# A spectral mixer with an MLP: stages one and two issued from lists of single steps, and the scale's sums in one bank

## The chip, the cores and the metric

The kernel runs on one core of a Trainium2 chip. The metric is device time in microseconds, from one execution of the whole program. The times of several runs are given by their median; the profile is of one execution, whose own time stands beside its span.

## The reference

The input x has 2048 rows of 512. Six vectors (sa, ca, ga, sb, cb, gb) of 512 come from silu(c) @ w_mod, c being one vector of 512. Two residual blocks follow, cut here to what matters:

```python
h = layernorm(x) * (1 + ca) + sa
X = rfft2(h) * (w_r + 1j * w_i)            # over the 2048 rows and the 512 columns
x = x + ga * irfft2(X)
h = layernorm(x) * (1 + cb) + sb
a = mish(h @ w1 + b1)                      # 512 to 1376
x = x + gb * (a @ w2)                      # 1376 to 512
```

All inputs and outputs are float32.

## The kernel before, in words

The row index is 16p + n for the 128 partitions p and 16 tiles n, so that one tile n holds 128 rows. The two-dimensional transform is made of small matmuls in three stages, and the MLP belongs to the third.

**Stage one** (lines 357 to 439) goes over the 16 tiles. For tile n it takes the row transform of x by four products with kr (`p1_row`, the products on L269), subtracts the mean (`p1_mean`, L284, VectorE), scales by the inverse deviation and splits the result into a high and a low part (`p1_cast`, L291 to L300 on ScalarE; the low part on GpSimd, L298, for odd n up to 13, else on VectorE in `p1_low`, L307). Then `p1_col` does the first part of the column transform in three parts of three matmuls (L314 to L316), the third of which needs the low part, and `p1_save` (L320) puts it into `a_sb`. The column matrices come as float32 and are split by `p1_split` (L261 on ScalarE, L262 and L263 on GpSimd). The statistics are `norm_sums` (L183, L184), `first_guess` (L188, L189) and `first_scale` (L196). Two buffers in PSUM of each of four tags (A, B, C, D) go round: the row products use A and B, the column products C.

Before the first tile, the factor 1 + ca is worked into kr: `gate` makes silu(c) (L377 to L380), `scale_sums` (L322 to L326) multiplies the columns of w_mod (`wmc`) with it, in four banks of 128 equal columns, and `scale_rows` (L328 to L331) makes four slices `krs` = kr * sum + kr on VectorE, each from its own bank. The shift sa is summed at the end of stage one (`shift_sum`, L176) and goes through the row transform in `shift_rows` (L336 to L350).

**Stage two** (lines 643 to 697) goes over 17 groups of up to four of the 64 frequency columns; group 0 is a special one (`z_...`). A group is transposed on TensorE (`p2_in`, L539), copied to SBUF (L542), shifted (L550, GpSimd), multiplied by the constant kf (`p2_mul`, L559), multiplied pointwise with the filter (`p2_prod`: two lane copies on ScalarE L590 and L591, GpSimd L592, VectorE L593), added (`p2_add`, L599), multiplied by kv (`p2_out`, L608) and stored (`store_d`, L450 to L458) by three engines. The last group's product is on VectorE alone (L583 to L586). Between the groups VectorE makes column sums of w_mod (`mod_late`, L176), and the gate ga goes through memory (`flat`, `spread`, L99 and L103) into kiv (`mod_gate`, L635, GpSimd).

**Stage three** (from line 1163) has the last two transforms (`p3_col`, L859 and L860; `p3_row`, L869) and the MLP, with its weights and activations as high and low parts and a seven-product scheme for two-by-two blocks (`up`, L974 and L991; `down`, L1091).

**What sets the order.** The kernel schedules by hand: every engine does its instructions in the order in which the program issues them, and DMAs go into the queue of the engine that issues them (mostly SyncE, SP). In stages one and two this order is written as loops with fixed leads. In stage three each step is put into a `Plan` with a key, the steps are sorted by key, and the list `ORDER` says in which order the sorted steps are issued (L1165 to L1176).

Of the kernel before, what the change touches and what calls it, by code (L numbers as in the profile page):

```python
# [12 lines left out]
P = 128  # L13
S, D, F = 2048, 512, 1376
L = D // 2 + 1
N2 = 16
# [17 lines left out]
ORDER = (  # L34
# [49 lines left out]
def tile_spectral_block(ctx: ExitStack, tc: tile.TileContext, x_d, w1_d, b1_d, w2_d,  # L84
# [157 lines left out]
    def load_all(n):  # L242
        load_xt(n)
        load_x(n)
        load_m(n)

    def load_rest():
        nc.sync.dma_start(kf, kf_d)
        nc.sync.dma_start(wz, wz_d)
        for i in range(4):  # L250
            nc.sync.dma_start(wqa[:, i], wq_d[i])
            if i == 1:
                nc.sync.dma_start(kv, kv_d)
                nc.sync.dma_start(kw, kw_d)
                nc.sync.dma_start(kiv, ki_d)
                nc.sync.dma_start(b1n[:, 0:NF - 1], b1_d[0:(NF - 1) * P].rearrange("(f p) -> p f", p=P))
                nc.sync.dma_start(b1n[0:F - (NF - 1) * P, NF - 1:NF], b1_d[(NF - 1) * P:F].unsqueeze(1))

    def p1_split(n):
        m = mt(n)  # L260
        nc.scalar.copy(m[:, 0, 0:256], mraw[:, n, :])  # L261
        nc.gpsimd.tensor_tensor(m[:, 1, 0:256], mraw[:, n, :], plain(m[:, 0, 0:256]), op=ALU.subtract)  # L262
        nc.gpsimd.tensor_scalar(m[:, :, 256:384], plain(m[:, :, 128:256]), -1.0, 0.0,  # L263
                                op0=ALU.mult, op1=ALU.add)
# [12 lines left out]
    def row_sums():  # L277
        ps = bank("D")
        row_products(ps, lambda j: ones)
        nc.scalar.copy(kb, ps)  # L280
# [6 lines left out]
    def p1_cast(n):  # L287
        c = st["c", n]
        one = rstd[:, n:n + 1]
        gh, gl = buf("g1", F32R), buf("g2", F32R)  # L290
        if n in POOL_LOW:  # L291
            g = buf("t")
            if n == 1:
                nc.scalar.activation(gh, c, AF.Copy, scale=one)
            nc.scalar.activation(g, c, AF.Copy, scale=one)
            if n > 1:
                nc.scalar.copy(gh, g)
            nc.gpsimd.tensor_tensor(gl, g, plain(gh), op=ALU.subtract)  # L298
        else:
            nc.scalar.activation(gh, c, AF.Copy, scale=one)  # L300
        st["g", n] = gh, gl

    def p1_low(n):
        c = st.pop(("c", n))
        if n not in POOL_LOW:
            gh, gl = st["g", n]
            nc.vector.scalar_tensor_tensor(gl, c, rstd[:, n:n + 1], plain(gh), op0=ALU.mult, op1=ALU.subtract)  # L307
# [1211 lines left out]
```

## Time and profile before

| | us |
|---|---|
| median of 3 runs (368.21 to 368.68) | 368.21 |
| the profiled execution's own time | 368.36 |
| its span | 366.6 |
| TensorE busy (PE) | 358.6 |
| VectorE (DVE) | 302.5 |
| ScalarE (ACT) | 266.9 |
| GpSimd (POOL) | 78.3 |

The span runs from the first to the last instruction; the time around it is outside of what the profile shows. TensorE's busy time is made of modelled ends of pipelined matmuls; PEld is its loading of weights, which goes on beside it. In the rows below, L followed by a number is a line of the kernel above, and the arrow in brackets names what ended a wait.

### The profile page before, as it was taken

The page shows a single profiled execution, that of the slowest core. Times are in us where ns is not written, and L with a number is a line of the kernel's source. Part 1 is how long each engine was busy: PE and PEld are TensorE (multiplying, and loading weights), DVE is VectorE, ACT ScalarE, POOL GpSimd, SP SyncE. Part 2 cuts the span into 40 slices and gives each one's busy share as a digit, 9 for nine tenths or more (in the row PEclk, how much of TensorE's full clock was granted, in tenths as well). Part 3 has the DMA queues.
Part 4 walks back from the last instruction along what each step waited for, and adds up shares of the span by engine and source line. Part 5 has one row for each costly group of instructions (what it writes and reads, how often), then busy time and mean ns, then how long its engine had stood idle before and what let it go on. Part 6 is the DMA issues. An engine that isn't in the chain of part 4 may idle for free.

```text
span 366.6 us, 7820 instructions
## 1 busy us (share of the span) xinstructions
PE 358.6 (98%) x2666; PEld 333.9 (91%) x2666; DVE 302.5 (83%) x752; ACT 266.9 (73%) x601; POOL 78.3 (21%) x126
## 2 busy tenths in 40 slices
PE   8999999998999999999999999999999999999994
PEld 8999977777999998798999999999999999999994
DVE  1898968888889799998994777998759977887995
ACT  1798879996799999998773878766577753555650
POOL 0588738786011001100002101004100000000000
PEclk9999999999999999999999999999999999999998
DMA  7999997678498776899888877786989678863133
GB/s 254 383 349 377 331 373 250 219 185 305 142 327 254 236 256 230 278 306 322 248 225 292 276 236 200 207 276 206 281 301 243 215 229 266 227 219 62 59 57 115
DMA packets 54343, 89.96 MB, mean 245 GB/s; under 512 B 7552, under 2 KB 20960, under 8 KB 54048
## 3 DMA queue, kind: packets, MB, share of 16 engines
q1 hardware_dynamic: 49728, 74.65, 62.0%
q0 software_dynamic: 2416, 7.87, 9.0%
q10 hardware_dynamic: 2160, 6.95, 6.0%
q8 instruction: 21, 0.34, 0.4%
q14 instruction: 18, 0.15, 0.1%
HBM read 68.21 MB, written 17.57 MB: 234 GB/s over the span
## 4 chain that ended last, share of the span: by engine, by line
PE 84%; ACT 5%; DVE 4%; DMA 2%; POOL 1%; issue 1%; ACTq 1%; SPq 0%; DVEq 0%; POOLq 0%
PE bank L1091 25%; PE bank L991 22%; PE bank L974 6%; PE bank L269 4%; PE bank L869 4%; PE bank L859 3%; PE bank L860 3%; PE bank L1037 3%; PE bank L314 3%; PE bank L1087 3%; DMA hT<-in_B_w_dram 2%; PE bank L1103 2%; PE bank L316 1%; PE bank L315 1%; PE bank L325 1%
## 5 line engine op out<-in xcount | busy, mean ns | idle before, releaser
L991 PE MATMUL bank<-hT,wr 128*128 128x256 f32 x360 | 51.6, 283 | 0.0
L991 PEld LDWEIGHTS bank<-hT,wr 128*128 128x128 f32 x360 | 47.3, 191 | 0.6
L991 PE MATMUL bank<-hB,wr 128*128 128x256 f32 x318 | 46.6, 285 | 0.0
L991 PEld LDWEIGHTS bank<-hB,wr 128*128 128x128 f32 x318 | 41.9, 191 | 0.9
L1143 POOL DMA_DIRECT2D x<-modr x7 | 6.3, 898 | 140.5 <-DVE modr L1142 84.7
L1091 PE MATMUL bank<-w2a,ah 128*128 128x256 f32 x161 | 35.1, 283 | 0.0
L917 DVE TENSOR_TENSOR al<-buf,ah 128x512 fp32r<-128x512 f32 (+1 forms) x45 | 30.1, 668 | 5.7 <-ACT ah L916 4.7
L1091 PE MATMUL bank<-w2b,ah 128*128 128x256 f32 x147 | 32.2, 283 | 0.0
L916 ACT CAST ah<-buf 128x512 fp32r<-128x512 f32 (+1 forms) x45 | 27.0, 602 | 4.5 <-DVE buf L1061 2.6
L1091 PEld LDWEIGHTS bank<-w2a,ah 128*128 128x128 f32 x161 | 27.0, 191 | 0.4
L859 PE MATMUL bank<-kc,d 128*128 128x128 f32 x128 | 24.9, 276 | 0.5 <-ACT d L452 0.5
L1091 PEld LDWEIGHTS bank<-w2b,ah 128*128 128x128 f32 x147 | 24.9, 191 | 0.3
L860 PE MATMUL bank<-kc,d 128*128 128x128 f32 x128 | 24.8, 275 | 0.0
L974 PE MATMUL bank<-hB,wr 128*128 128x512 f32 x96 | 24.4, 393 | 0.0
L1091 PE MATMUL bank<-w,ah 128*128 128x256 f32 x112 | 21.5, 284 | 0.0
L314 PE MATMUL bank<-buf,mring 128*128 128x512 f32 x48 | 20.6, 430 | 0.2 <-DVE buf L307 0.2
L974 PEld LDWEIGHTS bank<-hB,wr 128*128 128x128 f32 x96 | 17.3, 189 | 3.1
L859 PEld LDWEIGHTS bank<-kc,d 128*128 128x128 f32 x128 | 19.4, 192 | 0.7 <-ACT d L452 0.7
L860 PEld LDWEIGHTS bank<-kc,d 128*128 128x128 f32 x128 | 19.5, 192 | 0.0
L1091 PEld LDWEIGHTS bank<-w,ah 128*128 128x128 f32 x112 | 17.7, 191 | 0.6
L608 PEld LDWEIGHTS bank<-kv,a_sb 128*128 128x128 f32 x126 | 15.5, 192 | 2.8 <-issue 2.2
L788 POOL DMA_DIRECT2D turned<-x x16 | 8.9, 568 | 42.1 <-DVE x L782 42.1
(310 smaller groups left out, 1098.2 us busy)
## 6 DMA issues: line engine op xcount, KB each, us to landing
wr<-w_S SPq DMA_DIRECT2D x60, 256.0 KB, 4.0
wr<-w_A SPq DMA_DIRECT2D x45, 256.0 KB, 3.8
w_S<-hT SPq DMA_DIRECT2D x20, 256.0 KB, 2.9
x<-in_A_x_dram SPq DMA_DIRECT2D x16, 256.0 KB, 4.7
xring<-in_x_t_dram SPq DMA_DIRECT2D x16, 256.0 KB, 4.6
w_A<-wr SPq DMA_DIRECT2D x15, 256.0 KB, 3.1
x<-modr POOLq DMA_DIRECT2D x7, 512.0 KB, 5.5
out_dram<-x SPq DMA_DIRECT2D x7, 512.0 KB, 3.8
```

The lines of the kernel that those rows point to most:

```text
L269: nc.tensor.matmul(pgv[:, j], data(j), krs[:, j, :].rearrange("p (c q) -> p c q", c=2), start=True, stop=True)
L314: nc.tensor.matmul(pa, m[:, a, 0:128], g, start=(i == 0), stop=False)
L608: nc.tensor.matmul(pd[:, i * P:(i + 1) * P], y[:, i * P:(i + 1) * P], kv[:, 0:128], start=True, stop=True)
L859: nc.tensor.matmul(o, dj[:, 0:128], kc[0][:, n, :], start=True, stop=False)
L860: nc.tensor.matmul(o, dj[:, 64:192], kc[1][:, n, :], start=False, stop=True)
L869: nc.tensor.matmul(px[:, j * P:(j + 1) * P], e[:, j * P:(j + 1) * P], kiv[:, j, :], start=True, stop=True)
L916: nc.scalar.copy(h, r)
L917: nc.vector.tensor_tensor(l, r, plain(h), op=ALU.subtract)
L974: nc.tensor.matmul(ups[i, t, f], ring[t, a][:, p, b, :], sides[int(a[2]) - 1][:, :, q, b, :], start=(a[2] == "1" and b == 0 and n == 0), s ...
L991: nc.tensor.matmul(o, w[:, p, k, :], h[:, q, k, :], start=(first and n == 0), stop=(last and n == 5), skip_group_check=True)
L1037: nc.tensor.matmul(ups[i, 0][:FL], w1s[:, p, u, :], sides[u // 2][:, :, q, u % 2, :], start=(u == 0 and p + q == 0), stop=(u == 3 and p == ...
L1091: nc.tensor.matmul(out_ps[b][n][:, 256 * half:256 * half + 256], a[p][:, e], w2[t][q][:, r], start=(t == 1 and half == 0 and i == 0), stop ...
```

## The change

Four things are done.

1. Stages one and two become plans like stage three. The loops are cut into single steps (a load, a split's three parts, one part of a column product, one lane copy, one half of a store), which are put into `opening` and `middle` in the old order, roughly, and issued in the order of two new lists of 302 and 268 steps. The work of each engine stays on it, except for item 3.
2. Stage three gets a new list as well, for the same 1187 steps. Of these, half move by six places or fewer.
3. The scale's sums: one bank and 64 equal columns for each of the four slices in place of four banks of 128. The 1 is added once, to the four sums together (`scale_ones`), and the four slices are plain products with it, two on VectorE and two on ScalarE.
4. `shift_pick`, a reduction of the identity, is a step of its own.

The core of the diff, without the lists and without steps that are only cut out of their functions:

```diff
-    def scale_sums(ks, ps):
-        for k in ks:
-            for j in range(4):
-                nc.tensor.matmul(ps[j][:, 0:P], wmc[:, k, j * P:(j + 1) * P], sc[:, k:k + 1].to_broadcast([P, P]),
-                                 start=(k == 0), stop=(k == 3))
-    def scale_rows(ps):
+    def scale_sums(k):
+        if k == 0:
+            st["one"] = bank("C")
+        ps = st["one"]
         for j in range(4):
-            nc.vector.scalar_tensor_tensor(krs[:, j, :], kr[:, j, :], ps[j][:, 0:1], kr[:, j, :],
-                                           op0=ALU.mult, op1=ALU.add)
+            nc.tensor.matmul(ps[:, 64 * j:64 * j + 64], wmc[:, k, j * P:(j + 1) * P], sc[:, k:k + 1].to_broadcast([P, 64]),
+                             start=(k == 0 and j == 0), stop=(k == 3), skip_group_check=True)
+
+    def scale_ones():
+        ps = st.pop("one")
+        st["one"] = one = small.tile([P, 4], F32, name="one")
+        nc.vector.tensor_scalar(one, ps[:, 0:256:64], 1.0, None, op0=ALU.add)
+
+    def scale_row(j):
+        one = st["one"][:, j:j + 1]
+        if j % 2:
+            nc.scalar.activation(krs[:, j, :], kr[:, j, :], AF.Copy, scale=one)
+        else:
+            nc.vector.tensor_scalar(krs[:, j, :], kr[:, j, :], one, None, op0=ALU.mult)
...
+        def run(self, which):
+            steps = [e[2:] for e in sorted(self, key=lambda e: e[:2])]
+            places = [[int(n) for n in run.split("-")] for run in ORDERS[which].split()]
...
+    with tc.manual_schedule():
+        opening.run(0)
...
+        middle.run(1)
...
-    plan.run()
+    plan.run(2)
```

The places in the new lists that the prediction speaks of, by engine (`a > b` means that a is issued before b):

- SP: wmc's first quarter > sc > the other quarters > kr > x 0 > xt 0 > xt 1. At the end of stage one: three of wqa's four loads > kiv > kf > wz.
- VectorE, stage one: `scale_ones` > `scale_row` 0 and 2 > `norm_sums` 0 > ... > `norm_sums` 3 > `shift_pick` > `p1_mean` 2.
- TensorE, stage one: `p1_col` 1, first part > `p1_row` 5 > `p1_col` 1, the rest > `p1_row` 4 > `p1_col` 2, two parts > `p1_row` 7 > `p1_col` 2, third part. Before: `p1_row` 4 > `p1_col` 1, third part > `p1_col` 2 > `p1_row` 5.
- ScalarE, stage two: kc's two loads > copies of groups 12 and 13; lanes of groups 14 and 15 > store of group 10 > store of group 11 > `gate_spread`.
- VectorE, end of stage two: `own` 15 > `p2_add` 14 > `lane` 16 twice > `own` 16 > `p2_add` 15 > `p2_add` 16 > three `mod_late`. Before: `p2_add` 14 > `own` 15 > `lane` 16 > `p2_add` 15 > `lane` 16 > `own` 16 > `p2_add` 16 > two `mod_late`.
- TensorE, start of stage three: `p3_col` 0, 1 > `p3_row` 0, 1 > `p3_col` 2, 3 > `p3_row` 2 > `p3_col` 4 > `p3_row` 3, and so on. Before: `p3_col` 0, 1 > `p3_row` 0 > `p3_col` 2 > `p3_row` 1, 2 > `p3_col` 3, 4 > `p3_row` 3.

More of the change, by code (lines that the diff above doesn't have):

```diff
@@ L240, in load_xt, with p1_high, p1_rest, p1_minus @@
         st["xt", n] = t
[L242 to L259, printed above, removed]
+    def p1_high(n):
+        nc.scalar.copy(mt(n)[:, 0, 0:256], mraw[:, n, :])
+    def p1_rest(n):
         m = mt(n)
-        nc.scalar.copy(m[:, 0, 0:256], mraw[:, n, :])
         nc.gpsimd.tensor_tensor(m[:, 1, 0:256], mraw[:, n, :], plain(m[:, 0, 0:256]), op=ALU.subtract)
+    def p1_minus(n):
+        m = mt(n)
         nc.gpsimd.tensor_scalar(m[:, :, 256:384], plain(m[:, :, 128:256]), -1.0, 0.0,
@@ L297, in p1_cast, with p1_col @@
                 nc.scalar.copy(gh, g)
[L298 to L301, printed above, removed]
     def p1_low(n):
         c = st.pop(("c", n))
-        if n not in POOL_LOW:
-            gh, gl = st["g", n]
+        gh, gl = st["g", n]
+        if n in POOL_LOW:
+            nc.gpsimd.tensor_tensor(gl, st.pop(("gt", n)), plain(gh), op=ALU.subtract)
+        else:
             nc.vector.scalar_tensor_tensor(gl, c, rstd[:, n:n + 1], plain(gh), op0=ALU.mult, op1=ALU.subtract)
-    def p1_col(n, part=range(3)):
+    def p1_col(n, i):
@@ L336, in shift_rows @@
     def shift_rows():
-        ps = bank("D")
+        st["shift"] = ps = bank("D")
         pgv = ps.rearrange("p (c d q) -> p d c q", c=2, d=4)
@@ L380, in tile_spectral_block @@
         nc.vector.tensor_tensor(sc, sc, sg, op=ALU.mult)
-        warm(6)
-        cps = [bank(t) for t in "CCBB"]
-        for k in range(4):
-            scale_sums((k,), cps)
-        scale_rows(cps)
-        row_sums()
-        norm_sums(0)
-        first_guess(0, 1)
-        first_scale(0, 1)
-        p1_split(0)
-        p1_row(0)
-        load_all(8)
-        p1_row(1)
-        load_all(9)
-        scale_spread()
-        p1_mean(0)
-        p1_cast(0)
-        norm_sums(1)
-        first_guess(1, 2)
@@ new lines, in tile_spectral_block @@
+    put(load, sc, c_d.rearrange("b (p k) -> p (b k)", k=4))
+    put(table)
+    for k in range(4):
+        put(load, wmc[:, k, :], wm_d[1, k])
+    put(load, kr, kr_d)
+    put(load_xt, 0)
+    put(load_x, 0)
+    put(load_m, 0)
+    put(load_xt, 1)
+    put(load, ident, kp_d)
+    for n in range(1, 8):
+        put(load_x, n)
+        put(load_m, n)
+        if n < 7:
+            put(load_xt, n + 1)
+    put(set_ones)
+    put(gate)
+    put(warm, 6)
+    for k in range(4):
+        put(scale_sums, k)
@@ new lines, in tile_spectral_block, with split_steps, load_steps, rest_steps @@
+    put(scale_ones)
+    for j in range(4):
+        put(scale_row, j)
+    def split_steps(n):
+        put(p1_high, n)
+        put(p1_rest, n)
+        put(p1_minus, n)
+    def load_steps(n):
+        put(load_xt, n)
+        put(load_x, n)
+        put(load_m, n)
+    def rest_steps():
+        put(load, kf, kf_d)
+        put(load, wz, wz_d)
+        for i in range(4):
+            put(load, wqa[:, i], wq_d[i])
+            if i == 1:
+                put(load, kv, kv_d)
+                put(load, kw, kw_d)
+                put(load, kiv, ki_d)
+                put(load, b1n[:, 0:NF - 1], b1_d[0:(NF - 1) * P].rearrange("(f p) -> p f", p=P))
+                put(load, b1n[0:F - (NF - 1) * P, NF - 1:NF], b1_d[(NF - 1) * P:F].unsqueeze(1))
@@ new lines, in tile_spectral_block @@
+    put(p1_row, 0)
+    put(row_sums)
+    put(row_copy)
+    put(norm_sums, 0)
+    put(first_guess, 0, 1)
+    split_steps(0)
+    load_steps(8)
+    put(p1_row, 1)
+    load_steps(9)
+    put(scale_spread)
+    put(p1_mean, 0)
+    put(first_scale, 0, 1)
+    put(p1_cast, 0)
+    put(norm_sums, 1)
+    put(first_guess, 1, 2)
+    split_steps(1)
+    put(spread_copy)
+    put(p1_low, 0)
+    put(p1_mean, 1)
+    put(first_scale, 1, 2)
+    split_steps(2)
+    put(p1_cast, 1)
+    put(p1_low, 1)
@@ new lines, in tile_spectral_block @@
+    put(norm_sums, 2)
+    for n in range(N2):
+        if n >= 1 and n != 2:
+            put(p1_save, n - 1)
+        if n + 2 < N2:
+            put(p1_row, n + 2)
+            if n == 2:
+                put(p1_col, 1, 2)
+                put(p1_save, 1)
+            if n + 10 < N2:
+                load_steps(n + 10)
+            if n == 4:
+                put(load, wms, wm_d[0].rearrange("k p e -> p k e"))
+            if n == 6:
+                rest_steps()
+        if 1 <= n and n + 1 < N2:
+            put(p1_mean, n + 1)
+            if n % 2:
+                put(first_scale, n + 1, n + 3)
+            put(p1_cast, n + 1)
+            if n + 1 in POOL_LOW:
+                put(p1_low, n + 1)
+        for i in range(n + 2 + (n > 5), min(n + 3 + (n > 4), N2)) if n else ():
+            split_steps(i)
+        if n and n not in POOL_LOW:
+            put(p1_low, n)
+        for i in range(2) if n == 1 else range(3):
+            put(p1_col, n, i)
+        if n + 3 < N2:
+            put(norm_sums, n + 3)
+            if n % 2 == 0:
+                put(first_guess, n + 2, n + 4)
+        if 11 <= n < 15:
+            put(shift_sum, n - 11)
@@ new lines, in tile_spectral_block, with store_d @@
+    put(p1_save, N2 - 1)
+    put(shift_rows)
+    put(shift_pick)
+    for lo, hi in ((0, 16), (16, NQ)):
+        put(shift_own, lo, hi)
+    with tc.manual_schedule():
+        opening.run(0)
+    dd = [big.tile([P, 8, 4, 3, NQ], F32, name=f"d{i}", tag=t) for i, t in enumerate(("da", "db"))]
+    def store_d(g, i, part, kind):
+        q0, nq = groups[g]
+        src = st["pd", g][:, 0:nq * 128].rearrange("p (q a c) -> p a c q", q=nq, c=2)
+        dst = dd[i].rearrange("p n d c q -> p (n d) c q")
+        s = src[:, 32 * i:32 * i + 32]
+        to, minus = dst[:, :, 0:2, q0:q0 + nq], dst[:, :, 2, q0:q0 + nq]
+        if part == 0:
@@ L609, in p2_out @@
                              start=True, stop=True)
-        store_d(pd, q0, nq, "all" if nq < 4 else kind)
-    late = {}
+    late, second, kc = {}, [], []
     work_mod = {s: [] for s in range(len(seq) + 6)}
@@ L631, in mod_second, with second_in, gate_flat, gate_spread @@
         return w
+    def second_in(k):
+        second.append(mod_second(k))
+    def gate_flat():
+        st["ga"] = flat("ga", gcol[:, 0])
+    def gate_spread():
+        spread(modr[:, 0], st["ga"])
     def mod_gate():
@@ new lines, in z_zero, with put, in_steps, prod_steps @@
+    def z_zero():
+        nc.gpsimd.memset(z_space()[1][0:96, 0:P], 0.0)
+    middle = Plan()
+    def put(fn, *args):
+        middle.at(len(middle), fn, *args)
+    def in_steps(g, shift=True):
+        put(turn_z, g)
+        put(copy_z, g)
+        if shift and g:
+            put(p2_shift, g)
+    def prod_steps(g):
+        if g == 0:
+            return put(z_prod)
+        for half in range(2):
+            put(lane, g, half)
+        if g != seq[-1]:
+            put(other, g)
+        put(own, g)
@@ new lines, in tile_spectral_block @@
+    for i in range(4, 8):
+        put(load_wq, i)
+    for s in range(1, 4):
+        for w in work_mod[s]:
+            put(mod_fetch, *w)
+    for i in range(LEAD):
+        in_steps(seq[i], i > 1)
+        if i == 1:
+            for g in seq[:2]:
+                put(p2_shift, g)
+        if i in (2, 4):
+            put(p2_mul, seq[i // 2 - 1])
+            if i == 4:
+                put(p2_add, seq[0])
+            prod_steps(seq[i // 2 - 1])
+    for s in range(1, len(seq) + 3):
+        for w in work_mod.get(s + 3, ()):
+            put(mod_fetch, *w)
+        if 2 <= s < len(seq) + 2 and seq[s - 2] and groups[seq[s - 2]][0] < 32:
+            put(load_wq, groups[seq[s - 2]][0] // 4 + 8)
+        if s <= 15:
+            for w in work_mod[s]:
+                put(mod_late, *w)
+        if s + 2 == len(seq):
+            put(p2_mul, seq[-1])
+            put(lane, seq[-1], 0)
+            put(p2_add, seq[s])
+            put(lane, seq[-1], 1)
+            put(own, seq[-1])
+        elif s < len(seq) and seq[s]:
+            put(p2_add, seq[s])
+        if s + 2 < len(seq):
+            put(p2_mul, seq[s + 1])
+            prod_steps(seq[s + 1])
+        for i in ((), (5,), (6, 7), ())[s] if s < 4 else (s + 4,):
+            if i < len(seq):
+                in_steps(seq[i])
+        if s > 15:
+            for w in work_mod[s]:
+                put(mod_late, *w)
+        if s == 2:
+            put(z_zero)
+        if s == len(seq):
+            for k in range(2):
+                put(second_in, k)
+        if s == 5:
+            put(z_back)
+            put(z_rows)
+        if s >= 3:
+            g = seq[s - 3]
+            put(p2_out, g)
+            kind = "all" if s > 15 or groups[g][1] < 4 else "pool" if s > 13 else "busy" if work_mod[s] else "free"
+            for i in range(2):
+                put(store_d, g, i, 0, kind)
+                put(store_d, g, i, 1, kind)
+        if s == 11:
+            put(gate_flat)
+        if s == 13:
+            put(gate_spread)
+        if s == 16:
+            put(mod_gate)
+        if s in (11, 12):
+            put(load_kc, s - 11)
```

300 lines of the change are left out of this document (96 added, 204 removed), and 109 rows, old and new, of tables (ORDER, ORDERS).

## The prediction

> **What bounds the kernel now.** I read the page first, then the stretches (busy time by engine), then the chain of waits, then the timelines of TensorE and its feeders where the chain leaves TensorE.
>
> ```profile
> span 366.6 us, 7820 instructions
> PE 358.6 (98%) x2666; PEld 333.9 (91%) x2666; DVE 302.5 (83%) x752; ACT 266.9 (73%) x601; POOL 78.3 (21%) x126
> PE 84%; ACT 5%; DVE 4%; DMA 2%; POOL 1%; issue 1%; ACTq 1%; SPq 0%; DVEq 0%; POOLq 0%
> ```
>
> TensorE holds 84% of the chain. A reordering removes no matmul, so it can win only where TensorE stands still, and that has to be counted by stage. A busy TensorE in the stretches is no proof that it is dense, because matmul ends are modelled; the distance from start to start is.
>
> ```profile
> 20.28 0.89 PE bank L269 x8
> 22.59 0.89 PE bank L269 x8
> 8.58 1.23 PE L269 MATMUL bank<-modr,ones 128*128 128x128 f32 x8
> 49.66 1.72 PE L539 MATMUL bank<-ident,a_sb 128*128 128x128 f32 x11
> ```
>
> **Stage one** (chain, then TensorE's timeline). One row of x, that is one `p1_row` of 0.89 and one `p1_col`, takes 22.59 - 20.28 = 2.31 us when TensorE is dense. From the sums of kr's rows (8.58) to the first transpose of stage two (49.66) lie 41.1 us; the work in them is 16 x 2.31 + 3 x 0.89 (row sums, spread, shift rows) = 39.6. So 1.5 us of stillness there, most of it before 20 us, where VectorE is the one that is late:
>
> ```profile
> 15.00:20.00 5.00, 4.82 (x33) 4.06 (x31) 4.83 (x13) 4.36 (x10) 3.43 (x5) 1.00 1.06 379
> 20.00:48.00 28.00, 27.99 (x203) 26.00 (x202) 25.87 (x68) 23.69 (x55) 22.05 (x30) 1.00 1.02 348
> 19.54 0.50 PE L314 MATMUL bank<-buf,mring 128*128 128x512 f32 x1 [0.18 <-DVE buf L307]
> ```
>
> The columns are PE, PEld, DVE, ACT, POOL, then clock, DMA share, GB/s. VectorE is at 4.83 of 5, the clock is full, and VectorE needs 25.87 of the 28 us that follow: it is nearly as tight as TensorE.
>
> **Stage two** (TensorE's timeline).
>
> ```profile
> 69.36 1.06 PE L608 MATMUL bank<-kv,a_sb 128*128 128x128 f32 x8
> 71.55 1.06 PE L608 MATMUL bank<-kv,a_sb 128*128 128x128 f32 x8
> 90.01 0.49 PE L859 MATMUL bank<-kc,d 128*128 128x128 f32 x2 [0.46 <-ACT d L452]
> 49.60:90.00 40.40, 38.86 (x240) 28.42 (x239) 33.92 (x73) 36.33 (x88) 30.15 (x52) 1.00 0.78 265
> 84.50:90.00 5.50, 4.18 (x32) 3.64 (x31) 5.02 (x11) 3.99 (x16) 3.62 (x6) 1.00 0.82 308
> ```
>
> A dense group of four columns takes 71.55 - 69.36 = 2.19 us; seventeen of them (the first has three columns and the zero group is made otherwise; I count both as whole groups, an estimate) make 37.2. From 49.66 to 90.01 lie 40.35, so 3.1 us of stillness: 1.3 at the tail (5.50 - 4.18), the rest at the head, while the first groups go once round all engines, and in the last step to stage three. ScalarE has 36.33 of work in this stage, so it is the second bound.
>
> **Stage three** has nothing to give except at its start:
>
> ```profile
> 90.00:362.00 272.00, 271.61 (x2088) 260.59 (x2088) 230.46 (x576) 195.93 (x436) 20.18 (x32) 1.00 0.74 228
> 140.00:160.00 20.00, 20.00 (x104) 16.73 (x103) 19.77 (x53) 19.74 (x51) 2.16 (x4) 1.00 0.81 276
> 97.77 1.16 PE L869 MATMUL bank<-kiv,buf 128*128 128x128 f32 x8 [0.35 <-ACT buf L862]
> ```
>
> The second row (DVE 19.77 and ACT 19.74 of 20) is the tightest place of the kernel. The third is a `p3_row` that stood 0.35 us for its copy. **The ceiling** of all reordering is thus about 1.5 + 3.1 + 0.4 = 5 us, 1.4%.
>
> **The change, part by part.**
>
> *The scale's sums in 64 columns.* 16 products, two passes each:
>
> ```profile
> 4.21 4.53 PE bank L325 x32
> L325 PEld LDWEIGHTS bank<-sc,wmc 128*128 128x128 f32 x32 | 4.4, 223 | 0.5 <-issue 0.5
> L476 PEld LDWEIGHTS bank<-kf,early 128*1 128x1 f32 x2 | 0.1, 82 | 0.2 <-issue 0.2
> L269 PEld LDWEIGHTS bank<-modr,xring 128*128 128x128 f32 x128 | 15.6, 192 | 0.0
> ```
>
> The moving side is halved, the weights (128 columns of wmc) are not. No row has 64 moving columns. From below: half of a dense pass of 0.89 / 8 = 0.111 us, 0.056; from above: 0.111, if loading weights sets the pace. The weight-load rows decide: 128 columns of weights take 192 - 82 = 110 ns longer than one column, which is the whole pitch. So I take 0.111, a gain of nothing; the other end is worth 32 x 0.055 = 1.8 us and is rival 2.
>
> [...]
>
> *One bank, and 1 + s as a step of its own.* Today the first row of kr is scaled while TensorE still sums the other banks:
>
> ```profile
> 8.11 1.16 DVE L330 SCALAR_TENSOR_TENSOR modr<-kr,bank 128x128 f32<-128x128 f32 x4 [4.87 <-PE bank L325]
> 9.19 0.68 DVE L183 BATCH_NORM_STATS2 st<-x 128x6 f32<-128x512 f32 x1
> L378 DVE TENSOR_SCALAR sg<-sg 128x4 f32<-128x4 f32 x1 | 0.2, 170 | 1.7 <-ACT sg L377 1.7
> L470 ACT COPY early<-bank 128x128 f32<-128x128 f32 x1 | 0.3, 265 | 0.0
> ```
>
> L330 starts at 8.11, before the sums end (4.21 + 4.53 = 8.74), and `row_sums` follows at 8.58. Afterwards: sums end 8.74, `scale_ones` (nearest row 0.17) to 8.96, `scale_row` 0 between 0.17 and 0.35, say 0.28, so `row_sums` at about 9.3, 0.7 later. This is a new wait at the head of VectorE's queue: behind `scale_ones` stand the rows of kr and `norm_sums` 0, and TensorE's first three row products wait for them. The rows on two engines (0.265 on ScalarE, two of 0.28 on VectorE in place of 1.16) let `norm_sums` of row 0 start at about 9.5, 0.3 later than 9.19.
>
> *The loads.* SP now issues wmc's first quarter ahead of sc:
>
> ```profile
> 0.72 0.39 SPq L358 DMA_DIRECT2D sc<-in_c_dram  x1
> 1.18 2.90 DMA wmc<-in_w_mod_dram
> 2.42 0.20 ACT L377 ACTIVATE sg<-sc 128x4 f32<-128x4 f32 x1 [0.42 <-DMA sc<-in_c_dram]
> ```
>
> wmc lands 0.46 earlier (4.08 becomes 3.6), sc between 0.46 later (2.9) and behind the quarter on the same queue (3.6); the gate's four small steps take about 0.8 (an estimate from L377's 0.20 and L378's 0.17 with their hand-overs). The sums start between 3.7 and 4.4; I take the present 4.2. Every other load of stage one keeps its place to within a few; kf, kv and wqa come after x and are not needed before 51.
>
> *The order of stage one.* I wrote out both lists by engine. VectorE's begins in the same order, with `shift_pick` (0.4, today in TensorE's shadow at the end) put ahead of `p1_mean` 2. TensorE now does rows 5 and 7 before the third part of column 2. Today row 5 follows it, at 20.28. So when that part runs, some 0.7 us later (0.3 and 0.4, from 19.54 to 20.2), TensorE has 2 x 0.89 = 1.8 us more behind it: ahead by 1.1 us. VectorE, 0.7 later with 2.1 us of slack in the next 28, gives part of that back. I take half: **-0.6** for stage one, bounds +1.1 (all delays, no credit) and -1.5 (all stillness).
>
> *Stage two.* Work stays on its engines; only order changes. At the tail:
>
> ```profile
> 82.00 0.37 ACT L452 COPY d<-bank 128x256 f32<-128x256 f32 x1
> 82.39 0.59 ACT L590 ACTIVATE buf<-bank 64x512 f32<-64x512 f32 x1
> 85.41 0.69 DVE L599 TENSOR_TENSOR a_sb<-bank,buf 128x512 f32<-128x512 f32 x1
> 87.58 0.69 DVE L599 TENSOR_TENSOR a_sb<-bank,wide 128x512 f32<-128x512 f32 x1
> 88.19 0.68 DVE L176 SCALAR_TENSOR_TENSOR wm<-wm,bank 128x512 f32<-128x512 f32 x1
> ```
>
> The lanes of group 15 (82.39) go ahead of the store at 82.00: 0.39 earlier. One more column sum of w_mod (0.68 and 0.08) moves behind the last `p2_add` (87.58): up to 0.76 less on VectorE before it. Against this the add of group 15 (85.41) moves behind group 16's products, right ahead of the last add, so `p2_out` 15 and 16 and their stores run back to back: about 0.3 late. Net -0.5. The head keeps its order but for one transpose drawn forward; I count nothing. **-0.5**, bounds +0.8 and -3.1. Late there: `gate_spread` on ScalarE's queue moves behind the stores of group 11, from 81.03 to about 84 (82.39 - 0.39 + two lanes of 0.59 + two stores of 0.37), and the gated kiv is needed at 93.7:
>
> ```profile
> L869 PE MATMUL bank<-kiv,buf x24: 274/275/377, 93.7 to 98.7; 128*128 128x128 f32 x24
> 81.03 0.33 ACTq L103 DMA_DIRECT2D modr<-ga  x1
> 88.92 1.54 POOL L635 TENSOR_TENSOR kiv<-kiv,modr 128x512 f32<-128x512 f32 x1 [1.88 <-DMA modr<-ga]
> modr<-gb ACTq DMA_DIRECT2D x1, 256.0 KB, 4.8
> ```
>
> It took 7.9 us behind kc's two loads on that queue. Those now go ahead of the copies of groups 12 and 13, so I take the 4.8 of its twin: 84 + 4.8 + 1.5 = 90.3, in time. At 7.9 it would be 93.4, 0.8 late for a first `p3_row` drawn forward by 1.1. `gate_flat` goes forward too, to the stores of the zero group, which wait on ScalarE if the fourth gate sum is late; that sum moves forward with it. POOL issues no DMA before stage three.
>
> *Stage three.* Of its 1187 steps half move by six places or fewer. The start has two columns ahead of each row product, which removes the 0.35 at 97.77. **-0.3**, bounds -0.4 and +2 (below).
>
> **Sum:** 368.36 (the profiled execution: span 366.6 and 1.8 around it) - 0.6 - 0.5 - 0.3 = 366.96, **367.0**. The median of the runs is 368.21, 0.15 less than the profiled one; the forecast is 0.33% under it.
>
> **The rivals.**
>
> 1. *The longer start is never repaid: slower.* Row sums 0.7 late, `shift_pick` 0.4 more on VectorE, which stays the bound to the end of stage one (25.87 of 28 speaks for it), and the tight stretch from 140 to 160 loses one VectorE step of 0.7 by its new order: +1.8, less the tail's 0.5: 369.6. It decides where the third part of column 2 starts later than 20.2 by more than the 1.1 us of rows drawn forward. Against it: those rows need only xt, which lands in time at 379 GB/s. 0.18.
> 2. *Weights don't set the pace, the sums are half as long* (1.8 less): they end at about 7, `row_sums` at 7.6, but row 0 then waits for xt, issued at 4.00 and 4.6 under way (rows below), until 8.6; today it starts behind the row sums at 8.58 + 0.89 = 9.5, so about 1.0 more gain: 366.0. Against it: the 110 ns. 0.12.
>
> ```profile
> 4.00 0.43 SPq L239 DMA_DIRECT2D xring<-in_x_t_dram  x1
> xring<-in_x_t_dram SPq DMA_DIRECT2D x16, 256.0 KB, 4.6
> ```
>
> 3. *No net change*: ScalarE (36.33 of 40.4) paces stage two and what stage one gains is waited for there, or kiv comes 0.8 late: 368.2. 0.15.
> 4. The forecast: 0.55.
>
> **Chances.** About 0.2% (0.7 us) is what a measurement of this kernel can tell from no change, so faster means below 367.5. From the forecast 0.45 and rival 2: faster 0.57; rival 3 and the forecast's weak end: same 0.24; rival 1 and a little: slower 0.19. The range goes from 365.3, under rival 2, to 369.2, into rival 1; about one in ten lies out on either side.
>
> **What would show it.** Right: `row_sums` near 9.3, sums still 4.5 long, the third part of column 2 with two more rows done before it, stage two starting near 49.0, p3 near 88.9, no wait at the first `p3_row`s. Wrong: sums of 3 us; a wait of POOL for modr past 90; waits in 140 to 160; stage two longer than 40.4.

## The result, and the profile after

The changed kernel takes **372.67 us** in the median of 20 runs (367.76 to 373.77), the kernel before 368.43 (367.58 to 370.08, 20 runs). The ratio is 1.0077, 95% interval 1.0048 to 1.0106: slower. The forecast was 367.0 us, with a range up to 369.2.

The 20 times do not lie round their median. Four are 367.8 to 368.0, three 370.7 to 371.0, thirteen 372.4 to 373.8; I call the first short and the last long executions. The profile that came with the result is of a short one (367.76 us). Of the same kernel, run again, a long one was profiled (373.22 us; E1 below). Two disturbed executions, of 707 us (one of twelve of E13, with the only profile of E13) and of 588 us (the kernel before beside E13 to E15), are left out of what is said below.

The heads of the two pages, first the short one:

```profile
span 365.7 us, 7802 instructions
PE 356.8 (98%) x2666; PEld 333.2 (91%) x2666; DVE 302.5 (83%) x751; ACT 266.3 (73%) x603; POOL 77.6 (21%) x126
...
PE 82%; DVE 6%; ACT 3%; POOL 2%; DMA 2%; issue 2%; ACTq 0%; SPq 0%; DVEq 0%; POOLq 0%
```

and the long one:

```profile
span 371.1 us, 7802 instructions
PE 362.6 (98%) x2666; PEld 339.0 (91%) x2666; DVE 302.6 (82%) x751; ACT 266.4 (72%) x603; POOL 77.5 (21%) x126
```

The same 2666 matrix instructions keep TensorE busy 5.8 us longer, and VectorE, ScalarE and POOL not at all (within 0.1). So the long execution does not wait longer: its matmuls take longer. Which ones, TensorE's timeline shows (start, length, line, count, idle time before). The short execution of the changed kernel:

```profile
4.34 3.79 PE L336 MATMUL bank<-sc,wmc 128*128 128x64 f32 x32 [0.37 <-DVE sc L413]
8.71 1.16 PE L276 MATMUL bank<-modr,ones 128*128 128x128 f32 x8 [0.58 <-DVE modr L349]
9.70 1.95 PE L276 MATMUL bank<-modr,xring 128*128 128x128 f32 x16
11.49 1.06 PE L190 MATMUL bank<-ident,sc 128*128 128x128 f32 x8
...
48.88 1.72 PE L621 MATMUL bank<-ident,a_sb 128*128 128x128 f32 x11
...
89.33 0.49 PE L989 MATMUL bank<-kc,d 128*128 128x128 f32 x2 [0.46 <-ACT d L542]
```

The long one:

```profile
1.04 2.93 PE L377 MATMUL bank<-ones 128*128 128x128 f32 x12 [1.04 <-DVE b1n L406]
4.33 7.09 PE L336 MATMUL bank<-sc,wmc 128*128 128x64 f32 x32 [0.36 <-DVE sc L413]
12.00 2.08 PE L276 MATMUL bank<-modr,ones 128*128 128x128 f32 x8 [0.58 <-DVE modr L349]
13.87 3.62 PE L276 MATMUL bank<-modr,xring 128*128 128x128 f32 x16
17.28 1.16 PE L190 MATMUL bank<-ident,sc 128*128 128x128 f32 x8
...
54.68 1.72 PE L621 MATMUL bank<-ident,a_sb 128*128 128x128 f32 x11
```

The same order, the same waits, but 7.09 for 3.79, 2.08 for 1.16, 3.62 for 1.95: a pass takes 0.22 us in place of 0.11, up to about 17 us. From there on all is 5.8 us later (54.68 against 48.88). Twelve us at half speed (0.22 us a pass in place of 0.11), from 5 to 17, cost 6: that is the loss, of which the later stages give back 0.4 (the spans differ by 5.4). The stretches do not say so (busy time with count, granted clock, DMA share, GB/s). Short, then long:

```profile
5.00:6.00 1.00, 1.00 (x12) 1.00 0.86 297
16.00:17.00 1.00, 1.00 (x12) 1.00 1.08 395
```

```profile
5.00:6.00 1.00, 1.00 (x7) 1.00 0.94 342
16.00:17.00 1.00, 1.00 (x6) 1.00 1.05 398
17.00:18.00 1.00, 1.00 (x9) 1.00 1.04 401
```

TensorE is busy all the time and the clock column says 1.00 in both; in these rows only the count of passes in a microsecond tells half speed (6 or 7) from full (9 to 12). The column prints 1.00 also where the trace holds no record of the clock; what is on record is told below. The kernel before has the half speed too, but only to between 5 and 6:

```profile
5.00:6.00 1.00, 1.00 (x7) 1.00 1.00 354
7.00:8.00 1.00, 1.00 (x11) 1.00 1.08 364
```

### The profile page after: what moved, and what is told of

Same layout as the page of the kernel before. It is cut to its first block, busy times and chain, and to the rows that moved or that the text cites. A ratio compares the mean times of both kernels' runs of the same rounds, so it can differ in the third digit from the quotient of the medians.

```text
span 365.7 us, 7802 instructions
## 1 busy us (share of the span) xinstructions
PE 356.8 (98%) x2666; PEld 333.2 (91%) x2666; DVE 302.5 (83%) x751; ACT 266.3 (73%) x603; POOL 77.6 (21%) x126
## 4 chain that ended last, share of the span: by engine, by line
PE 82%; DVE 6%; ACT 3%; POOL 2%; DMA 2%; issue 2%; ACTq 0%; SPq 0%; DVEq 0%; POOLq 0%
PE bank L1221 24%; PE bank L1121 22%; PE bank L1104 6%; PE bank L276 4%; PE bank L999 3%; PE bank L324 3%; PE bank L1167 3%; PE bank L990 3%; PE bank L989 3%; PE bank L1217 3%; DMA hT<-in_B_w_dram 2%; PE bank L325 2%; PE bank L326 2%; PE bank L645 1%; PE bank L336 1%
## 5 line engine op out<-in xcount | busy, mean ns | idle before, releaser
L1121 PE MATMUL bank<-hB,wr 128*128 128x256 f32 x318 | 45.5, 284 | 0.0
```

What stands on the lines that cost most here:

```text
L1121: nc.tensor.matmul(o, w[:, p, k, :], h[:, q, k, :], start=(first and n == 0), stop=(last and n == 5), skip_group_check=True)
```

## The experiments

**Which part costs.** Theories at first: a late load, in stage three (its new list) or in stages one and two; against them, the sums themselves. Four kernels on one chip, the kernel before there at 368.22.

*E1*, the changed kernel unaltered.

> The changed kernel once more, unaltered. Its profiled execution took 367.76 us, 0.6 less than before, yet most of its 20 executions took 370.7 to 373.8. Theory 1 (the new list of stage three lets a step come due that waits for a load through memory, and in most executions that load is late): most executions again 370 to 374, and a profile of such a one shows one or two waits for a DMA of 3 to 5 us after 90 us. Theory 2 (the new lists of stages one and two move loads so that they collide): the same times, but the wait stands before 90 us. If the profile falls on an execution of 368 it tells nothing between them.

372.57 us (12 runs), ratio 1.0090 (1.0056 to 1.0123), four executions under 369.2 and eight over 372.3. Its profile is the long one above: the loss lies ahead of 17 us, where no load that the theories named is waited for.

*E2*, the changed kernel with the old list of stage three:

```diff
-    "3-4 1-2 0 16 15 5 90 7 21 47 56 14 8 12 6 79 38 10 88 13 17 9 19 92 26 24 96 11 20 22 27 23 33 25 18 28-29 36 "
...
+    "0 3-4 1-2 16 15 5 7 21 90 47 56 88 8 10 12 92 6 64 19 79 38 13 24 14 96 11 17 20 22 27 23 29 98 18 33 32 9 54 "
...
```

> The changed kernel with the old list for stage three; stages one and two and the scale's sums as changed. Theory 1: all executions 367 to 368, none over 369. Theory 2: most executions 370 to 374, as for the whole change.

372.51, ratio 1.0098 (1.0065 to 1.0131): the loss stays.

*E3*, the kernel before with the new list of stage three alone (the same edit the other way).

> The kernel before with the new list for stage three alone. Theory 1: most executions 371 to 374. Theory 2: 368 to 369 in all executions, like the kernel before.

367.87, ratio 0.9996 (0.9982 to 1.0010): neither loss nor gain.

*E4*, the kernel before with the new way to the scale alone: 64 columns, one bank, `scale_ones`, rows on two engines.

```diff
-                nc.tensor.matmul(ps[j][:, 0:P], wmc[:, k, j * P:(j + 1) * P], sc[:, k:k + 1].to_broadcast([P, P]),
+                nc.tensor.matmul(ps[:, 64 * j:64 * j + 64], wmc[:, k, j * P:(j + 1) * P], sc[:, k:k + 1].to_broadcast([P, 64]),
...
-            nc.vector.scalar_tensor_tensor(krs[:, j, :], kr[:, j, :], ps[j][:, 0:1], kr[:, j, :],
...
+    nc.vector.tensor_scalar(one, ps[:, 0:256:64], 1.0, None, op0=ALU.add)
```

> The kernel before with the scale's sums alone changed: 64 columns, one bank, one addition, rows on two engines. By the prediction the 32 passes keep 0.111 us each and the row sums start 0.7 us later than 8.58, near 9.3; the whole time rises by 0 to 0.7 us. If weights do not set the pace, the 32 passes take about 2.7 us instead of 4.5 and the row sums start before 8.

372.38, ratio 1.0077 (1.0042 to 1.0112), the whole loss (four executions of ten at 368.0 to 368.6, six at 372.3 to 373.4), and its profiled execution shows it at the same place:

```profile
3.94 7.06 PE L325 MATMUL bank<-sc,wmc 128*128 128x64 f32 x32
11.58 2.08 PE L269 MATMUL bank<-modr,ones 128*128 128x128 f32 x8 [0.58 <-DVE modr L335]
13.45 3.62 PE L269 MATMUL bank<-modr,xring 128*128 128x128 f32 x16
```

Both theories of a late load fall: here all loads and lists are those of before.

**Columns or bank?** Four kernels, the kernel before at 368.23.

*E5*, the three new lists with the old sums and rows. 
```diff
-        ps = st["one"]
+        st["one"] = [bank(t) for t in "CCBB"]
...
-            nc.tensor.matmul(ps[:, 64 * j:64 * j + 64], wmc[:, k, j * P:(j + 1) * P], sc[:, k:k + 1].to_broadcast([P, 64]),
+            nc.tensor.matmul(st["one"][j][:, 0:P], wmc[:, k, j * P:(j + 1) * P], sc[:, k:k + 1].to_broadcast([P, P]),
...
+        nc.vector.scalar_tensor_tensor(krs[:, j, :], kr[:, j, :], st["one"][j][:, 0:1], kr[:, j, :],
```

> The three new lists with the old sums and rows of the scale (128 columns, four banks, rows on VectorE). Theory A (TensorE's clock: while the 64-column passes run it stays at half speed in most executions): no execution over 370, median 367.0 to 367.9, since in the profiled execution of the change stage one was 0.8 shorter than before. Theory B (something in the new order of stage one is late by chance): a part of the executions at 370 to 373.

369.06, ratio 1.0022 (0.9999 to 1.0044). The loss of the 64 columns is gone, but theory A's expectation is missed: two of twelve executions lie over 370 (371.09 and 371.75), and the median is 1.2 over its upper end.

*E6*, the changed kernel with 128 columns in its one bank; *E8* is the same with 96 in place of P:

```diff
-            nc.tensor.matmul(ps[:, 64 * j:64 * j + 64], wmc[:, k, j * P:(j + 1) * P], sc[:, k:k + 1].to_broadcast([P, 64]),
+            nc.tensor.matmul(ps[:, P * j:P * j + P], wmc[:, k, j * P:(j + 1) * P], sc[:, k:k + 1].to_broadcast([P, P]),
...
-        nc.vector.tensor_scalar(one, ps[:, 0:256:64], 1.0, None, op0=ALU.add)
+        nc.vector.tensor_scalar(one, ps[:, 0:512:P], 1.0, None, op0=ALU.add)
```

> The change with 128 columns for each slice, still in one bank, with one addition and the rows on two engines. Theory A: no execution over 370, passes of 0.111 us, median 367.0 to 368.2. Theory C (four sums in one bank hold the passes up, not the clock): most executions at 370 to 373.

> The change with 96 columns for each slice in one bank. [...] Theory C: most executions at 370 to 373, whatever the columns.

E6: 368.99, ratio 1.0018 (0.9991 to 1.0045), six executions at 367.0 to 368.2 and six at 369.8 to 370.9. E8: 369.36, ratio 1.0015 (0.9990 to 1.0039), five executions over 370. That no execution of E6 would be over 370 was missed as well (five are): something besides the columns makes a second, smaller group.

*E7*, the kernel before with 64 columns in its four banks, nothing else:

```diff
-                nc.tensor.matmul(ps[j][:, 0:P], wmc[:, k, j * P:(j + 1) * P], sc[:, k:k + 1].to_broadcast([P, P]),
+                nc.tensor.matmul(ps[j][:, 0:64], wmc[:, k, j * P:(j + 1) * P], sc[:, k:k + 1].to_broadcast([P, 64]),
```

> The kernel before with 64 columns in place of 128 and nothing else: four banks, rows on VectorE, old lists. Theory A: most executions at 371 to 373, the profile with passes of 0.22 us well past 8 us. Theory C: all executions at 367 to 369.

371.80, ratio 1.0078 (1.0055 to 1.0101). The one bank is cleared; the width of the moving side alone makes the loss, and 96 columns no longer do (E8 is level with E6).

```profile
3.88 7.06 PE L325 MATMUL bank<-sc,wmc 128*128 128x64 f32 x32
10.72 2.02 PE L269 MATMUL bank<-modr,ones 128*128 128x128 f32 x8
12.54 2.25 PE L269 MATMUL bank<-modr,xring 128*128 128x128 f32 x16
```

That gave the theory that the rest tests, the clock theory: **TensorE starts at half speed (the first products take 0.24 us a pass, 2.93 / 12, where it takes 0.11 later), the products of the first microseconds bring the turn to full speed, and 64-column passes, which at half speed still take 0.22 us each (7.06 / 32) and so move half as many columns in that time, bring it later.** This is my inference from E4 to E8. The starting pace and the places of the turns are measured; what brings a turn about is not on record.

**The clock on record.** A trace keeps the granted clock as a list of intervals, and the views print 1.00 where it has none. In each of the 16 undisturbed profiles the first interval, at full clock, starts where the passes change from one every 0.213 us to one every 0.111: after 3.87 us in the short execution, 17.50 in the long one (E1), 5.73 in the kernel before. So it is the clock that differs. This interval at full clock is 361.813, 351.573 and 358.399 us long in these three.

| profile | columns of the sums | the sums: start, length | turn to full clock |
|---|---|---|---|
| before | 128 | 4.21, 4.53 | 5.73 |
| changed, short | 64 | 4.34, 3.79 | 3.87 |
| changed, long (E1) | 64 | 4.33, 7.09 | 17.50 |
| E4 | 64 | 3.94, 7.06 | 17.21 |
| E7 | 64 | 3.88, 7.06 | 13.16 |
| E6 | 128 | 4.56, 6.19 | 9.54 |
| E8 | 96 | 4.38, 5.80 | 8.59 |

With 128 and with 96 columns the turn comes while the sums run. With 64 it comes 2.2 to 6.2 us after their end in E1, E4 and E7, and ahead of them in the short execution. Time busy alone does not decide: from 4.33 to 11.42 of E1 TensorE runs 64-column passes without a gap, and the clock stays. The short execution and the long one have the same twelve passes of ones ahead (1.04, 2.93) and their sums start within 0.01 us of each other, and yet one turned at 3.87 and the other at 17.50; of the 40 executions of the changed kernel, E1 and E2, nine are under 369.2. What decides between the two is not shown, and neither is how much work brings a turn.

**More work as a test, and the idle time.** In the new lists sc comes after wmc's first quarter, and TensorE stands 0.36 to 0.59 us ahead of the sums (before, 0.24). A second theory: this gap, too, can delay the turn. In E6's profile (370.77 us, of the upper group) it is longest:

```profile
4.56 6.19 PE L336 MATMUL bank<-sc,wmc 128*128 128x128 f32 x32 [0.59 <-DVE sc L413]
```

The turn is on record at 9.54 us there, with the same columns as in the kernel before, where it is at 5.73. Four kernels, the kernel before at 368.29.

*E9*, the changed kernel with twelve products of ones ahead of the sums in place of six:

```diff
-    put(warm, 6)
+    put(warm, 12)
```

> The changed kernel with 64 columns and one bank, and with twelve instead of six plain 128-column products of ones ahead of the sums: more work, nothing else. Clock theory (TensorE starts at half speed; it turns to full speed only after it has been filled for long enough, and 64-column passes do not fill it, because they move half as many columns in the time that a weight load takes): the longer filled stretch, about 1.0 to 6 us, lets the turn come before or soon after the sums start, so no execution is over 371 and the median is between 367.5 and 369.5, under the changed kernel's 372.6 although 12 passes are added. Rival, the 64-column sums are slow in themselves: six more products at 0.49 us each delay everything by up to 3 us, 373 to 376.

369.15 (368.44 to 369.82, all 12 in one group), ratio 1.0023 (1.0011 to 1.0035). Twelve passes more, and 3.4 us less than the changed kernel's median in E1, though that was taken on another chip; by the ratios to the kernel before on each chip it is 0.7%.

```profile
1.04 5.47 PE L377 MATMUL bank<-ones 128*128 128x128 f32 x24 [1.04 <-DVE b1n L406]
6.32 3.71 PE L336 MATMUL bank<-sc,wmc 128*128 128x64 f32 x32
10.60 1.16 PE L276 MATMUL bank<-modr,ones 128*128 128x128 f32 x8 [0.57 <-DVE modr L349]
```

The 24 passes of 128 columns go at 0.23, and the same 64-column sums, started 2 us later, end 1.4 us earlier than in the long execution (10.03 against 11.42). The rival, that 64-column sums are slow in themselves, falls. On record the turn is at 6.36 us, in the long execution at 17.50. So with more work of full width ahead it came earlier, in these two profiles; that TensorE has to be filled, and for how long, the run does not show.

*E10*, the changed kernel with 128 columns and sc loaded first:

```diff
-    "32 2 0 3-4 34 1 5-6 ...
+    "32 0 2 3-4 34 1 5-6 ...
```

> The changed kernel with 128 columns in its one bank, and with sc loaded ahead of the first quarter of wmc as in the kernel before; all new orders else kept. Theory that the late sc leaves TensorE idle ahead of the sums (0.4 to 0.6 us in place of 0.15 to 0.24) and that this breaks the stretch which the clock needs in about half of the executions: all executions between 366.5 and 369, median about 367.3. Rival, the idle time has nothing to do with it (the new orders themselves cost): again two groups around 367.5 and 370, median near 369.

368.42, ratio 1.0006 (0.9996 to 1.0016). One group, 367.28 to 369.17: E6's upper group, up to 370.85, is gone, as the theory of the gap wants. But the median is 1.1 over what I expected; the orders bring nothing.

*E11*, the kernel before with wmc's first quarter ahead of sc. 
```diff
+        nc.sync.dma_start(wmc[:, 0, :], wm_d[1, 0])
         nc.sync.dma_start(sc, c_d.rearrange("b (p k) -> p (b k)", k=4))
...
-        for k in range(4):
+        for k in range(1, 4):
             nc.sync.dma_start(wmc[:, k, :], wm_d[1, k])
```

> The kernel before with one edit: the first quarter of wmc is issued ahead of sc. Theory of the idle time: sums start at 4.35 to 4.6 after 0.4 to 0.6 us of idle time, and about half of the executions lie 2 to 3 us higher, median 368.5 to 370. Rival: only the start moves, by 0.2 to 0.4 us, and the median stays within 368.2 to 368.7 in one group.

368.67, ratio 1.0017 (0.9998 to 1.0036): six executions at 367.5 to 368.3 and six at 369.0 to 370.1, with the sums at

```profile
4.34 4.34 PE L325 MATMUL bank<-sc,wmc 128*128 128x128 f32 x32 [0.37 <-DVE sc L381]
```

Two groups as expected, a little nearer together (their means differ by 1.9 us, not 2 to 3), and an interval that still holds no change: in favour of the gap, not proof of it.

*E12*, E10 with eight products of ones. 
```diff
-    put(warm, 6)
+    put(warm, 8)
```

> The same as the one with 128 columns and sc first, with eight products of ones in place of six, so that TensorE has no idle time between them and the sums (they end at about 5 us where the six end at 3.97). Clock theory: never a late turn to full speed, all executions in one group; the sums start up to 0.9 us later, of which the earlier turn gives back a part: median 367.0 to 368.0. Rival, the six products are enough and the sums' start is what counts: 0.5 to 0.9 slower than the one with six.

368.90, ratio 1.0013 (0.9997 to 1.0029), 367.5 to 369.7. That is 0.5 over E10 by the medians, the lower end of what the rival had; the two intervals overlap, so it is not shown that more products cost time, but they gain none, and the one group at 367.0 to 368.0 that the clock theory wanted did not come.

```profile
4.61 3.75 PE L336 MATMUL bank<-sc,wmc 128*128 128x128 f32 x32
```

**Which order gains, which gives back.** Three kernels, the kernel before at 367.93.

*E13*, E10 with stage two's code and order of before:

```diff
-        middle.run(1)
+        for i in range(LEAD):
+            p2_in(seq[i])
...
```

> The changed kernel with 128 columns in one bank, sc loaded first, new orders of stages one and three, and the code and order of stage two from the kernel before. If stage two's new order gives back what the others gain (in the profile of the one with sc first it took 40.9 us from the first transposes to p3, before 40.35): median 367.6 to 368.0 against 368.2 of before, a ratio of 0.998 to 0.9995. Rival, stage two's order is neutral and the other two bring nothing either: 368.2 to 368.5.

*E14*, the kernel before with stage two's new order alone (the same edit the other way).

> The kernel before with the new order of stage two alone. If it is stage two that gives back: 368.4 to 368.8, 0.2 to 0.5 over before, first transposes at about 49.66 and p3 0.1 to 0.5 later than 90.01. By the prediction's own term for stage two (-0.5): 367.7.

*E15*, the kernel before with stage one's new order alone (E13 with the old list of stage three).

> The kernel before with the new order of stage one alone (128 columns in one bank, 1 + s as its own step, rows on two engines, sc first). By the prediction's term for stage one (-0.6): 367.6, first transposes near 49.0. Rival, the one bank and the longer start eat the credit: 368.1 to 368.5, first transposes at 49.4 to 49.7.

E13: 368.31, ratio 1.0018 (1.0002 to 1.0033), the rival's value and slower than before, if by little. E14: 368.42, ratio 1.0011 (0.9999 to 1.0023). E15: 367.42, ratio 0.9997 (0.9984 to 1.0010). By the medians stage one's order gains 0.5 and stage two's costs 0.5, but both intervals hold 1, and E13, which should have been the best, is not: no version here is shown to beat the kernel before, and the medians alone do not settle the orders. The profiles do better, below.

## Why the prediction was wrong, step by step

**The step that failed** is in the sums in 64 columns: "So I take 0.111, a gain of nothing". The pace itself was right. At full speed the width does not change it: 32 passes take 3.71 with 64 columns (E9) and 3.75 with 128 (E12), so rival 2 was rightly refused. What was missing is that TensorE is not at full speed there (in the profile of before a pass takes 0.213 us until 5.73 us), and that with 64 columns the turn can come much later: E7, where the width alone changes, takes 371.80 us and has the turn to full clock at 13.16 us, and E1 has it at 17.50, in place of 5.73. It cost 5.8 us in the long execution; no rival had it, and the range ended 3.5 us below the result.

**The sign stood in quoted rows.** "The clock is full" was said of 15 to 20 us, where it is true; of the time before 5.73 us the clock column could not tell, since it prints 1.00 where nothing is on record. But the sums' row was 4.53 for 32 passes, 0.142 each against the dense 0.111, and their weight loads took 223 ns against 192 for the same 128 columns elsewhere. I used that row for the start and the end of the sums and took the mean for nothing.

**One bank and 1 + s.** `scale_ones` was priced 0.17 and took 0.16 (the first row here; the second is two rows of kr):

```profile
8.17 0.16 DVE L342 TENSOR_SCALAR one<-bank 128x4 f32<-128x4 f32 x1 [3.88 <-PE bank L336]
8.37 0.48 DVE L349 TENSOR_SCALAR modr<-kr,one 128x128 f32<-128x128 f32 x2
```

The step from the end of the sums to the first row product is 0.58, as worked out (8.74 to 9.3); the row sums came at 8.71 because in this execution the sums ended at 8.13. Right.

**The loads.** I took the sums' start at 4.2 within 3.7 to 4.4. They start at 4.34, and between 4.33 and 4.56 in the seven profiles with this order of loads and six products (E1, E2, E5, E6, E8, E11 and the one that came with the result): sc is the late one. The term was given a bound of +0.2 for the start alone; that a gap might cost more than its length (E6 against E10) was not thought of.

**The order of stage one.** The gain is there, but smaller than the sum had it. From row sums to stage two's first transposes lay 41.08 us; now 48.88 - 8.71 = 40.17, and 40.17 to 40.27 in all seven profiles with the new order, the new rows of kr and the clock at full speed by the row sums (E6, E8, E9, E10, E12, E15 and the short one; E5, with the old rows, has 40.94). That is 0.9, where 0.7 lost at the row sums and -0.6 in all asked for 1.3. The total came near in E15 (and nearer than that in the short execution):

```profile
8.88 1.16 PE L215 MATMUL bank<-modr,ones 128*128 128x128 f32 x8 [0.58 <-DVE modr L288]
...
49.13 1.73 PE L567 MATMUL bank<-ident,a_sb 128*128 128x128 f32 x11
```

49.13 against 49.66 is -0.53, the -0.6 of the sum, but by luck: the row sums are at 8.88 and not at 9.3 because the clock had turned at 4.98 us there, earlier than in the profile of before. Where the sums keep their length, as in E10, the row sums come at 9.2 as forecast, and only 0.2 is left:

```profile
9.20 1.16 PE L276 MATMUL bank<-modr,ones 128*128 128x128 f32 x8 [0.58 <-DVE modr L349]
...
49.47 1.72 PE L621 MATMUL bank<-ident,a_sb 128*128 128x128 f32 x11
```

**Stage two: +0.1 in place of -0.5.** The tail did what was worked out. Its last 5.5 us (busy times of PE, PEld, DVE, ACT, POOL):

```profile
83.83:89.33 5.50, 4.70 (x40) 4.32 (x38) 5.40 (x12) 3.96 (x16) 4.38 (x6) 1.00 0.45 145
```

0.80 of stillness where there were 1.32. But the whole stage is 40.45 long, before 40.35:

```profile
48.88:89.33 40.45, 38.67 (x240) 28.65 (x238) 33.65 (x73) 36.46 (x88) 30.77 (x52) 1.00 0.83 280
```

TensorE's waits in it are

```profile
65.17 1.10 PE L645 MATMUL bank<-buf,kf 128*128 128x512 f32 x2 [0.37 <-DVE a_sb L685]
...
78.58 1.10 PE L645 MATMUL bank<-buf,kf 128*128 128x512 f32 x2 [0.18 <-DVE a_sb L685]
...
79.98 1.10 PE L645 MATMUL bank<-wide,kf 128*128 128x512 f32 x2 [0.31 <-ACT buf L632]
...
86.85 2.02 PE L694 MATMUL bank<-kv,a_sb 128*128 128x128 f32 x16 [0.34 <-DVE a_sb L685]
```

The first three, 0.86 together, are `p2_mul` products that stand for VectorE and ScalarE, and the timeline of the kernel before lists no wait from its first transposes to 86. E14 shows them again, with the same 40.45; E10 has them too, and 40.91. So the failed term is "the head keeps its order but for one transpose drawn forward; I count nothing": the middle was not worked through, only its ends. The gated kiv was in time, earlier than forecast (82.91 for the issue, not 84, and done at 88.46, not 90.3):

```profile
82.91 0.33 ACTq L122 DMA_DIRECT2D modr<-ga  x1
```

```profile
86.91 1.55 POOL L727 TENSOR_TENSOR kiv<-kiv,modr 128x512 f32<-128x512 f32 x1 [0.24 <-DMA modr<-ga]
```

**Stage three: near nothing in place of -0.3.** The wait of 0.35 at 97.77 went, and one of 0.65 came:

```profile
99.22 1.16 PE L999 MATMUL bank<-kiv,buf 128*128 128x128 f32 x8 [0.65 <-ACT buf L992]
```

From p3 to the end it is 365.7 - 89.33 = 276.4, before 276.6, but the same stretch is 275.2 to 276.7 over the profiles, with the old list and with the new; and E3's ratio is 0.9996. Within what can be told.

**Together:** -0.8, +0.1 and -0.2 make the -0.9 by which the short execution's span is under the span before (365.7 to 366.6). But 0.7 of the -0.8 is not the orders': the clock turned earlier in this execution (3.87 against 5.73 us), and the sums took 3.79 in place of 4.53. E10, with all new orders, 128 columns and sc first, is nearest to the forecast's kernel without the loss of the 64 columns, and it takes 368.42 against 368.29, not 1.2 less. So two things were wrong: the width's effect on the clock, which makes the result slower, and, smaller, the gain of the orders, of which stage one gives 0.9 for 1.3 and stage two nothing.

## What to carry to other kernels

Before a matmul at the start of a kernel is made narrower, look where the clock turns. Here 64 columns in place of 128 moved the turn from 5.73 us to 13.16 in the profiles (E7), and six wide products more had it at 6.36 in place of 17.50 (E9 against E1): the cheaper-looking product cost 5.8 us in the long execution. Read speed at the start of a kernel from passes per microsecond, from the mean of equal instructions in two places, or from where the trace's first clock interval begins, and not from the busy share or a clock column that prints 1.00 where it has no record. When a new list of steps is priced, work through the middle of each stage as well as its ends, and look at all the times of a kernel before its profile: the profiled execution may be the untypical one.

## What the runs showed of the hardware that was not expected

- TensorE takes 0.22 to 0.24 us for a pass of 64 or of 128 columns at the start of every undisturbed profile and 0.11 to 0.12 later. The turn is on record at 5.73 us in the profile of before and at 17.50 in the long one of the changed kernel. The clock column prints 1.00 before it, too.
- The turn differs between executions of one kernel: 3.87 us in the short one of the changed kernel, 17.50 in the long one.
- With 64 columns for the sums the turn is on record at 13.16 us (E7), 17.21 (E4) and 17.50 (E1), with 128 at 5.73 (before) and 9.54 (E6, with an idle gap of 0.59 us ahead of the sums), with 96 at 8.59 (E8). That the columns count is inferred from these profiles; the short execution, with 64 columns and the turn at 3.87, is not explained by it.
- Six products added ahead made the changed kernel some 3.4 us faster (E9 against E1, on two chips).
- The same program takes times in separate groups (367.8 to 368.0 and 372.4 to 373.8). What sorts an execution into a group is not shown: the short and the long profile have the same products ahead of the sums (1.04, 2.93), and the sums' start is at 4.34 and 4.33.
